# Attention chunks of a fused attention + two-MoE kernel: score products, y products and state products regrouped, and new durations for its list scheduler

## The chip, the cores and the metric

One core of one Trainium2 chip. The metric is the device time of one execution in microseconds (us), the median of several runs. Engines: PE (matrix multiply; "PEld" is its weight load, which overlaps the products), DVE (vector), ACT (scalar), POOL (general), SP (issues the DMAs).

## The reference

Three layers on 4 batches, 8 heads, 768 steps, 48 dimensions. The first is a linear recurrence with a complex decay:

```python
for t in range(S):
    new_re = ar * S_re - ai * S_im
    new_im = ar * S_im + ai * S_re
    S_re, S_im = (new_re + einsum('bhd,bhe->bhde', k[t], v[t]), new_im)
    y[t] = einsum('bhd,bhde->bhe', q[t], S_re)
```

Then a dense layer of width 2048 with a leaky rectifier, (3072 x 384) @ (384 x 2048) @ (2048 x 384), and then a layer with 8 experts of width 1024, of which each token uses one or none. All in float32.

## The kernel before

The recurrence is cut into 24 chunks, six of 128 steps for each of four batches; the number of a chunk is s = 4c + b. A chunk has two parts.

- `elementwise(s)` (E) loads a, q and k of the chunk into a tile X (two buffers), turns the decay into phases and magnitudes on ACT and DVE (two kinds of scan, line 416), and multiplies q and k by them. The results go through DRAM to be laid out anew: SP issues kd<-QP and qd<-X (write), then kh<-kd and qh<-qd (read back), and then the load of X for the chunk after next.
- `attention(s)` (P) forms, for two groups g of four heads, the 128 x 128 scores ("at", 4 products), masks them on DVE into A, transposes k ("at" again, 4 transposes) and copies it on ACT into kT, adds up y = v'A + St'q in the PSUM tile y, and forms the state products kT'v in the PSUM tile sps (one buffer, `s_ps`), which DVE adds to the state St and multiplies by the decay (su, then St). The last four chunks (c = 5) form no transposes and no state products, the first four (c = 0) have no St'q and no su.

A float32 product takes two passes on the tensor engine, so four products show as eight instructions. The y products go out by `columns`: each has 32 stationary columns, and four of them lie side by side in the array.

Each two chunks give 256 tokens to `moe_block(m)` (M, 12 of them): 8 pairs of F-blocks, each with 18 "h" products of 256 columns, ACT copies, DVE rectifies and splits (hs, gh, gl), and 12 "acc" products of 394 columns. The dense weights are decoded (d) in the first 120 us or so. After the last M comes the expert stage (loads r, items I), whose pools open when the attention pools and those of the dense layer close.

The order of all these instructions is written by a list scheduler, `Plan.emit`: it goes through a planned time, in which each recorded instruction has a duration (its `cost`), and at each step gives every engine the ready instruction with the lowest priority number. The result is a fixed order on every engine, and each engine then works through its order, waiting where an operand is late. The durations only set the order. Priorities come from `do_E`, `do_P`, `do_M`, `do_d` with lists of hand-set offsets; a chunk has four steps, `pri(0)` to `pri(3)`, and between two steps lies about one F-block pair of M. The planned end of a DMA is its bytes at a given rate plus 2 us (1.1 before it and 0.9 behind).

Of the kernel before, what the change touches and what calls it, by code (L numbers as in the profile page):

```python
# [57 lines left out]

# ---------------------------------------------------------------- list scheduler
class Buf:  # L60
    """A tile that is allocated when its first instruction is emitted."""

# [12 lines left out]
class View:  # L75
    """An access pattern on a Buf, resolved when its instruction is emitted."""

# [77 lines left out]
def real(x):  # L155
    return x.ap() if isinstance(x, View) else x
# [6 lines left out]
class Slots:  # L163
    """Buffers of one tag, taken in the order in which their first instructions are issued."""

# [20 lines left out]
class Plan:  # L186
    """Orders recorded instructions by priority as their operands become ready."""

    label = ''
    after = ()  # L190
# [17 lines left out]
    def gate(self, ops, fn):  # L208
        """Runs `fn` between `ops` and the instructions that name its result in `after`."""
        return self.add("NONE", 0.0, fn, after=ops)  # L210
# [152 lines left out]

# ---------------------------------------------------------------- kernel
def moe_kernel(tc, a, qk, v, w_in, w_out, alpha, w_gs, w1, w2, nat, nat_v, out):
# [7 lines left out]
    def cols(x):  # L373
        return x.cols if isinstance(x, View) else 0
# [40 lines left out]
    def scan(o, x, y, init, op1):  # L415
        dve(o, cols(o), lambda: nc.vector.tensor_tensor_scan(  # L416
            out=real(o), data0=real(x), data1=real(y), initial=real(init), op0=ALU.mult, op1=op1), [x, y, init])

    def mm(o, l, r, start, stop):
        n = cols(o)  # L420
        dt = l.dtype
        if dt == F32R:
            cost = max(n, 256) / 2.4 + 2.5
        elif dt == BF16:
            cost = 30
        else:
            cost = 2 * (max(n, 128) / 1.2 + (6 if n <= 128 else 0) if n > 64 else 213)
        pl.add("PE", cost / 1e3, lambda: nc.tensor.matmul(real(o), lhsT=real(l), rhs=real(r), start=start, stop=stop,  # L428
                                                          skip_group_check=True),
               [l, r] + ([] if start else [o]), [o])  # L430
# [27 lines left out]
    with ctx:  # L458
# [106 lines left out]
        def elementwise(s, pri):  # L565
# [44 lines left out]
            for x, name in ((1, "k"), (0, "q")):  # L610
                n = 129 if x else 128
                if x:
                    P = pl.buf(e1, [128, 6, 129], F32, "QP")
                    ts(P[:, :, 128].rearrange("p (c g) -> p c g", c=2), bc(GG[:, 127:384:128], 2), -0.5, ALU.mult)
                else:
                    P = X[:, 2:4, :].rearrange("p c (g t) -> p (c g) t", g=3)
                tt(P[:, :, 0:128].rearrange("p (c g) t -> p c g t", c=2),
                   X[:, 5 + x, :].rearrange("p (o g t) -> p o g t", o=1, g=3).to_broadcast([128, 2, 3, 128]), cs4, ALU.mult)
                d_ = pl.buf(drb, [6, 128, n], F32, name + "d", bufs=3)
                h_ = pl.buf(qp, [96, H, n], F32, name + "h", bufs=2) if x else qhs[s % 2][0:96, :, :]  # L620
                dma(d_.rearrange("x p t -> x p t"), P, 396e3)
                pl.ops[-1].fn = (lambda d=d_, P=P: nc.sync.dma_start(d.ap().rearrange("x p t -> p x t"), P.ap()))
                dma(h_, d_, 396e3)
                pl.ops[-1].fn = (lambda d=d_, h=h_: nc.sync.dma_start(
                    h.ap(), d.ap().rearrange("x (i h) t -> (x i) h t", h=H)))
                qk_of[s, x] = h_ if x else qhs[s % 2]

        def attention(s, pri):
# [10 lines left out]
            y = pbuf(y_ps, [128, 3, 128], "y")  # L639
            m4 = mask.rearrange("p (o f) -> p o f", o=1).to_broadcast([128, 4, 128])  # L640
            for g in range(2):
                pl.pri = pri(2 * g)
                at = pbuf(at_ps, [128, 512], "at", bufs=2)
                for x in range(4):
                    mm(at[:, x * 128:(x + 1) * 128], kh[:, 4 * g + x, 0:128], qh[0:96, 4 * g + x, :], True, True)
                A = pl.buf(pp, [128, 4, 128], F32, "A", bufs=2)
                tt(A, at.rearrange("p (x t) -> p x t", x=4), m4, ALU.mult)
                if not last:
                    at = pbuf(at_ps, [128, 512], "at", bufs=2)
                    for x in range(4):  # L650
                        transpose(at[:, x * 96:x * 96 + 96], kh[:, 4 * g + x, 0:128], ident[0:96, 0:96])
                    kT = pl.buf(pp, [128, 4, 96], F32, "kT", bufs=2)
                    copy(kT, at[:, 0:384].rearrange("p (x d) -> p x d", x=4))
                pl.pri = pri(2 * g + 1)
                ops = []
                for t, off in ((g, 32 * g), (2, 32 - 32 * g)):
                    for inter in range(c > 0, -1, -1):
                        for x in range(4):
                            h = 4 * g + x
                            cs = slice(h * 64 + off, h * 64 + off + 32)  # L660
                            ops.append((y[32 * x:32 * x + 32, t, :],) + (
                                (St[:, b, cs], qh[:, h, :]) if inter else (vt[:, cs], A[:, x, :])))
                columns(ops, g == 0)
                if last:
                    continue
                sps = pbuf(s_ps, [128, 512], "sps")[0:96, :]
                for x in range(4):
                    h = 4 * g + x
                    mm(sps[:, x * 128:x * 128 + 128], kT[:, x, :], vt[:, (h - g) * 64:(h - g) * 64 + 128],
                       True, True)  # L670
                new = sps.rearrange("p (h e) -> p h e", h=4)[:, :, 80 * g:80 * g + 48]
                sv = St[0:96, b, g * 256:g * 256 + 256].rearrange("p (h e) -> p h e", h=4)[:, :, 16 * g:16 * g + 48]
                gc = kh[:, 4 * g:4 * g + 4, 128:129].to_broadcast([96, 4, 48])
                if c:
                    su = pl.buf(pp, [96, 4, 48], F32, "su")
                    tt(su, new, sv, ALU.add)
                    tt(sv, su, gc, ALU.mult)
                else:
                    tt(sv, new, gc, ALU.mult)
# [3 lines left out]

        def columns(ops, fresh):
            """Products of 32 columns each, four of which the tensor engine carries side by side."""
            def go():
                for n, (o, l, r) in enumerate(ops):
                    ins = nc.tensor.matmul(real(o), lhsT=real(l), rhs=real(r), start=fresh and n < 4,
                                           stop=n >= len(ops) - 4, skip_group_check=True)
                return ins  # L690

            pl.add("PE", 0.0745 * len(ops), go, [x for op in ops for x in op[1:]], [op[0] for op in ops])

# [60 lines left out]
        def disjoint(group, ins, last):  # L754
            """The rows of one indirect write are not those of another: only the last one waits for them."""
            for other in group:
# [154 lines left out]
        def rank_experts(spare):  # L911
            """Order of the experts by their counts so far, and the slots each of them gets."""
            cnt = spare[0:1, 32:32 + E]
# [28 lines left out]
        def start_of(n):  # L942
            """Reads an item's expert and its first slot into registers."""
            r, _, col = ITEMS[n]
# [162 lines left out]
        def count_items(tp):  # L1107
            """Lists the (expert, first slot) of every 256 tokens beyond the first cap[e] of expert e."""
            cnt = scratch(tp)[:, 0:E]
# [29 lines left out]
        def check_inputs(tp):  # L1139
            """Sets the flag of the general path."""  # L1140
            good = tiny(tp, [128, NCHK + NF], "good")
# [12 lines left out]
        def finish():  # L1154
            """Tokens beyond the slots of their expert, after the general path if an input needs it."""
            pl.live = True
# [47 lines left out]
        def general():  # L1204
            """x1 and the routing without any assumption on the values: the recurrence step by step."""
            st = ExitStack()
# [148 lines left out]
        def filler():  # L1355
            """A product of constants that keeps the tensor engine's clock up while it waits for the first real ones."""
            if not idle:
# [134 lines left out]
```

## Time and profile before

| | |
|---|---|
| median of 3 runs | 811.39 us (808.46 to 816.9) |
| span of the profiled execution | 807.5 us |
| median of the runs less this span | 3.9 us |
| PE busy | 738.8 us, 91% of the span |
| DVE busy | 604.8 us, 75% |
| ACT busy | 498.4 us, 62% |
| last y products issued | 632.7 us |
| PE clock granted, mean | 0.981 |

The profile has the span, from the first to the last instruction; the run's own time is not given beside it, so the sum is made against the span, and 3.9 us are added to come to the median. Matmuls overlap, so that the step from one start to the next, and not the duration of one, is what a product costs the engine.

### The profile page before, as it was taken

How to read it: one execution, taken by the hardware profiler on the slowest of the kernel's cores; microseconds unless marked ns; L12 is line 12 of the kernel's file. 1: busy time of each engine (PE TensorE's matmuls, PEld its weight loads, DVE VectorE, ACT ScalarE, POOL GpSimd, SP SyncE). 2: the span in 40 equal slices, each digit the busy share in tenths (PEclk: the TensorE clock that was granted, in tenths of full speed). 3: DMA queues.
4: the chain of work that ended last, by engine and by line, in shares of the span. 5: the costliest groups of instructions: out<-in, count | busy, mean ns of one | idle time of the engine just before them, and what ended most of it. 6: DMA issues, size and time to landing. Idle time of an engine off the chain costs nothing.

```text
span 807.5 us, 16491 instructions
## 1 busy us (share of the span) xinstructions
PE 738.8 (91%) x6322; PEld 698.8 (87%) x6322; DVE 604.8 (75%) x1460; ACT 498.4 (62%) x839; POOL 70.5 (9%) x118
## 2 busy tenths in 40 slices
PE   1689899989999998999999999989999999999993
PEld 0578789979889998999998998889999999899993
DVE  5979989978879897887867788677873473676741
ACT  7769759666847785577777567586652362555530
POOL 4000000100000010010100101001000203710110
PEclk9989999999999999999999999999999999999997
DMA  6585665767484776525334542535340432599400
GB/s 232 164 261 170 216 209 175 216 193 236 109 275 122 212 213 203 145 70 166 112 114 131 158 129 76 142 101 135 116 132 2 165 126 84 187 395 390 155 11 18
DMA packets 86983, 130.53 MB, mean 162 GB/s; under 512 B 8822, under 2 KB 60096, under 8 KB 86896
## 3 DMA queue, kind: packets, MB, share of 16 engines
q1 hardware_dynamic: 84336, 125.35, 50.9%
q0 software_dynamic: 2560, 4.05, 1.6%
q8 instruction: 52, 0.85, 0.5%
q14 instruction: 35, 0.29, 0.2%
HBM read 99.46 MB, written 31.29 MB: 162 GB/s over the span
## 4 chain that ended last, share of the span: by engine, by line
DVE 28%; PE 28%; DMA 25%; ACT 12%; issue 4%; SPq 1%; POOL 0%; POOLq 0%; ACTq 0%; DVEq 0%
PE h L428 13%; PE acc L428 12%; DMA X<-in_a 9%; DMA qd<-X 7%; DVE X L397 6%; DVE hs L405 3%; ACT X L385 3%; DVE X L416 3%; DVE X L405 3%; ACT L357 3%; DMA qh<-qd 2%; DVE gl L397 2%; ACT Rr L385 2%; DVE QP L397 1%; DVE chk L412 1%
## 5 line engine op out<-in xcount | busy, mean ns | idle before, releaser
L428 PE MATMUL h<-xhi,wih 128*128 128x256 f32 x576 | 168.3, 293 | 1.1 <-ACT wih L390 0.7
L428 PE MATMUL h<-xlo,wih 128*128 128x256 f32 x576 | 164.3, 285 | 0.3 <-DVE xlo L397 0.2
L428 PE MATMUL h<-xhi,wil 128*128 128x256 f32 x576 | 163.4, 284 | 0.0
L385 ACT ACTIVATE X<-X 128x384 f32<-128x384 f32 (+1 forms) x216 | 117.8, 558 | 66.7 <-DMA X<-in_a 44.3
L428 PE MATMUL acc<-woh,gh 128*128 128x394 f32 x384 | 135.4, 353 | 8.4 <-ACT gh L390 8.2
L428 PE MATMUL acc<-wol,gh 128*128 128x394 f32 x384 | 132.7, 346 | 0.0
L428 PE MATMUL acc<-woh,gl 128*128 128x394 f32 x384 | 130.8, 353 | 1.5 <-DVE gl L397 1.1
L428 PEld LDWEIGHTS h<-xhi,wih 128*128 128x128 f32 x576 | 110.0, 191 | 3.0 <-issue 1.0
L428 PEld LDWEIGHTS h<-xlo,wih 128*128 128x128 f32 x576 | 110.2, 191 | 0.8 <-DVE xlo L397 0.7
L428 PEld LDWEIGHTS h<-xhi,wil 128*128 128x128 f32 x576 | 110.2, 191 | 0.1
L405 DVE SCALAR_TENSOR_TENSOR hs<-hs,alp 128x256 f32<-128x256 f32 x192 | 86.6, 479 | 31.0 <-ACT hs L390 30.6
L390 ACT CAST gh<-hs 128x512 fp32r<-128x512 f32 x96 | 59.0, 615 | 68.2 <-DVE hs L405 61.0
L357 ACT ACT_TABLE_LOAD x77 | 98.8, 1283 | 1.2
L428 PEld LDWEIGHTS acc<-woh,gh 128*128 128x128 f32 x384 | 73.1, 191 | 12.7 <-ACT gh L390 11.2
L390 ACT COPY hs<-h 128x512 f32<-128x512 f32 x96 | 55.5, 578 | 45.0 <-PE h L428 41.8
L397 DVE TENSOR_TENSOR gl<-hs,gh 128x512 fp32r<-128x512 f32 x96 | 65.8, 686 | 18.5 <-ACT gh L390 18.2
L856 POOL DMA_INDIRECT lst<-tok,ix x24 | 26.5, 1106 | 605.4 <-DVE ix L401 601.8
L428 PEld LDWEIGHTS acc<-woh,gl 128*128 128x128 f32 x384 | 71.5, 191 | 6.0 <-DVE gl L397 5.0
L397 DVE TENSOR_TENSOR X<-X 128x768 f32<-128x768 f32 (+1 forms) x96 | 72.0, 751 | 5.9 <-ACT X L385 5.7
L428 PEld LDWEIGHTS acc<-wol,gh 128*128 128x128 f32 x384 | 73.5, 191 | 0.1
L428 PE MATMUL at<-qh,kh 96*128 96x128 f32 x384 | 54.4, 281 | 15.7 <-DMA qh<-qd 15.7
L428 PEld LDWEIGHTS at<-qh,kh 96*128 96x128 f32 x384 | 50.4, 195 | 17.6 <-issue 16.3
(186 smaller groups left out, 1406.0 us busy)
## 6 DMA issues: line engine op xcount, KB each, us to landing
r<-in_w SPq DMA_DIRECT2D x24, 512.0 KB, 6.3
r<-in_w SPq DMA_DIRECT2D x32, 384.0 KB, 9.6
kd<-QP SPq DMA_DIRECT2D x24, 387.0 KB, 4.6
kh<-kd SPq DMA_DIRECT2D x24, 387.0 KB, 3.7
X<-in_a SPq DMA_DIRECT2D x24, 384.0 KB, 5.6
X<-in_qk SPq DMA_DIRECT2D x24, 384.0 KB, 6.1
qd<-X SPq DMA_DIRECT2D x24, 384.0 KB, 4.1
qh<-qd SPq DMA_DIRECT2D x24, 384.0 KB, 5.0
```

The costliest lines, as they stand in the source:

```text
L357: nc.scalar.preload_act_table_set(o)
L385: lambda: nc.scalar.activation(real(o), real(i), f, **{k: real(x) for k, x in kw.items()}),
L390: lambda: nc.scalar.copy(real(o), real(i)), [i], [o])
L397: dve(o, cols(o), lambda: nc.vector.tensor_tensor(out=real(o), in0=real(x), in1=real(y), op=op), [x, y], late=late)
L405: dve(o, cols(o), lambda: nc.vector.scalar_tensor_tensor(out=real(o), in0=real(x), scalar=real(s), in1=real(y), op0=op0, op1=op1), [x, y, s])
L412: dve(o, cols(i), lambda: nc.vector.tensor_reduce(out=real(o), in_=real(i), axis=AX.X, op=op, apply_absolute_value=absolute), [i])
L416: dve(o, cols(o), lambda: nc.vector.tensor_tensor_scan(out=real(o), data0=real(x), data1=real(y), initial=real(init), op0=ALU.mult, op1=op ...
L428: pl.add("PE", cost / 1e3, lambda: nc.tensor.matmul(real(o), lhsT=real(l), rhs=real(r), start=start, stop=stop, skip_group_check=True), [l ...
L856: r = nc.gpsimd.indirect_dma_start(out=lst, out_offset=bass.IndirectOffsetOnAxis(ap=real(ix[:, t:t + 1].bitcast(U32)), axis=0), in_=toks[t ...
```

## The change

In `attention`, the loop over the two head groups is cut in three: first scores, mask and transposes of both groups (steps 0 and 1), then one call of `columns` with the y products of both groups (step 2, all St'q first and then all v'A), and then the state products of both groups (step 3). A state product moves 96 columns of v and not 128, and `new` is cut out of the narrower result. The number of tensor instructions stays the same.

The scheduler gets other durations: scans 2n-16 columns and not n, float32r products 13.5 ns and not 2.5 ns beside their columns, float32 products by the larger of moving and stationary columns, the four transfers through DRAM 650 KB and 520 KB worth of time and not 396 KB, and a stretch of n y products 0.3 + 0.0575 n us and not 0.0745 n. The lists of priority offsets stay as they were. Comments are taken out elsewhere.

```diff
     def scan(o, x, y, init, op1):
-        dve(o, cols(o), lambda: nc.vector.tensor_tensor_scan(
+        dve(o, 2 * cols(o) - 16, lambda: nc.vector.tensor_tensor_scan(
...
         if dt == F32R:
-            cost = max(n, 256) / 2.4 + 2.5
+            cost = max(n, 256) / 2.4 + 13.5
         elif dt == BF16:
             cost = 30
         else:
-            cost = 2 * (max(n, 128) / 1.2 + (6 if n <= 128 else 0) if n > 64 else 213)
+            cost = 2 * (max(n, math.prod(l.shape[1:])) / 1.2 + (6 if n <= 128 else 0))
...
-                dma(d_.rearrange("x p t -> x p t"), P, 396e3)
+                dma(d_.rearrange("x p t -> x p t"), P, 650e3)
...
-                dma(h_, d_, 396e3)
+                dma(h_, d_, 520e3)
...
+            As, kTs = [], []
             for g in range(2):
-                pl.pri = pri(2 * g)
+                pl.pri = pri(g)
                 at = pbuf(at_ps, [128, 512], "at", bufs=2)
...
-                pl.pri = pri(2 * g + 1)
-                ops = []
-                for t, off in ((g, 32 * g), (2, 32 - 32 * g)):
-                    for inter in range(c > 0, -1, -1):
+            pl.pri = pri(2)
+            ops = []
+            for inter in range(c > 0, -1, -1):
+                for g in range(2):
+                    for t, off in ((g, 32 * g), (2, 32 - 32 * g)):
                         for x in range(4):
                             h = 4 * g + x
                             cs = slice(h * 64 + off, h * 64 + off + 32)
                             ops.append((y[32 * x:32 * x + 32, t, :],) + (
-                                (St[:, b, cs], qh[:, h, :]) if inter else (vt[:, cs], A[:, x, :])))
-                columns(ops, g == 0)
-                if last:
-                    continue
+                                (St[:, b, cs], qh[:, h, :]) if inter else (vt[:, cs], As[g][:, x, :])))
+            columns(ops)
+            pl.pri = pri(3)
+            for g in range(0 if last else 2):
                 sps = pbuf(s_ps, [128, 512], "sps")[0:96, :]
                 for x in range(4):
                     h = 4 * g + x
-                    mm(sps[:, x * 128:x * 128 + 128], kT[:, x, :], vt[:, (h - g) * 64:(h - g) * 64 + 128],
+                    mm(sps[:, x * 128:x * 128 + 96], kTs[g][:, x, :], vt[:, h * 64 - 32 * g:h * 64 - 32 * g + 96],
                        True, True)
-                new = sps.rearrange("p (h e) -> p h e", h=4)[:, :, 80 * g:80 * g + 48]
+                new = sps.rearrange("p (h e) -> p h e", h=4)[:, :, 48 * g:48 * g + 48]
...
-            pl.add("PE", 0.0745 * len(ops), go, [x for op in ops for x in op[1:]], [op[0] for op in ops])
+            pl.add("PE", 0.3 + 0.0575 * len(ops), go, [x for op in ops for x in op[1:]], [op[0] for op in ops])
```

## Rows read from the trace of the kernel before

**Rows 1.** The page: busy time of each engine, and granted clock by slice.

```profile
PE 738.8 (91%) x6322; PEld 698.8 (87%) x6322; DVE 604.8 (75%) x1460; ACT 498.4 (62%) x839; POOL 70.5 (9%) x118
...
PEclk9989999999999999999999999999999999999997
```

**Rows 2.** Busy time by stage: time, then PE, PEld, DVE, ACT, POOL, clock, DMA.

```profile
50.00:634.00 584.00, 557.02 (x5029) 521.73 (x5028) 470.37 (x1152) 390.34 (x664) 22.89 (x21) 0.99 0.52 153
...
100.00:150.00 50.00, 48.31 (x402) 45.22 (x403) 46.90 (x120) 37.08 (x69) 2.28 (x2) 1.00 0.62 182
...
550.00:600.00 50.00, 49.59 (x480) 46.70 (x479) 37.90 (x95) 30.87 (x50) 2.08 (x2) 1.00 0.48 132
```

**Rows 3.** PE's waits from 50 to 634 us: total, times, longest.

```profile
PE at L428 <- DMA qh<-qd: 12.7, 8, 2.8
PE acc L428 <- ACT gh L390: 8.2, 9, 1.9
```

**Rows 4.** Chain that ended last, shares by line, of 50:590 and of 590:634.

```profile
by line: DMA X<-in_a 12.3%; DMA qd<-X 8.3%; DVE X L397 7.7%; DVE hs L405 5.0%; ACT X L385 4.9%; issue 4.6%; DVE X L416 4.2%; ACT L357 4.0%; DVE X L405 3.7%; DMA qh<-qd 3.6%; PE acc L428 3.6%; PE h L428 3.2%; DVE gl L397 3.1%; ACT Rr L385 2.
...
by line: PE h L428 41.1%; PE acc L428 40.3%; PE y L688 9.3%; DMA ids<-lst 7.2%; PE at L428 6.1%; ACT gh L390 1.2%; issue 0.3%; SPq L991 0.1%
```

**Rows 5.** PE in order of time, one group of a chunk: start, duration.

```profile
500.89 0.34 PE L428 MATMUL acc<-wol,gh 128*128 128x394 f32 x1
501.06 0.34 PE L428 MATMUL acc<-woh,gl 128*128 128x394 f32 x1
501.33 0.42 PE L688 MATMUL y<-qh,St 128*32 128x128 f32 x8
501.57 0.40 PE L688 MATMUL y<-A,vt 128*32 128x128 f32 x8
501.79 0.40 PE L688 MATMUL y<-qh,St 128*32 128x128 f32 x8
502.01 0.40 PE L688 MATMUL y<-A,vt 128*32 128x128 f32 x8
502.34 1.11 PE L428 MATMUL sps<-vt,kT 128*96 128x128 f32 x8
503.21 0.36 PE L428 MATMUL h<-xhi,wih 128*128 128x256 f32 x1
...
507.63 1.05 PE L428 MATMUL at<-qh,kh 96*128 96x128 f32 x8
508.52 0.49 PE L433 MATMUL at<-ident,kh 96*128 96x96 f32 x4
508.80 0.36 PE L428 MATMUL h<-xhi,wih 128*128 128x256 f32 x1
```

**Rows 6.** PE in the decode stage, products of 10 moving columns, and what follows.

```profile
94.69 0.73 PE L428 MATMUL at<-wgs,wt 128*128 128x10 f32 x6
95.28 0.89 PE L428 MATMUL at<-Ao,ident 128*128 128x384 f32 x2
```

**Rows 7.** Weight loads by shape: busy, mean ns of one, idle before.

```profile
L428 PEld LDWEIGHTS at<-qh,kh 96*128 96x128 f32 x384 | 50.4, 195 | 17.6 <-issue 16.3 <-DMA qh<-qd 1.3
L428 PEld LDWEIGHTS sps<-vt,kT 128*96 128x96 f32 x320 | 37.2, 163 | 5.9 <-issue 4.2 <-ACT Rr L385 0.6 <-ACT wih L390 0.4
L688 PEld LDWEIGHTS y<-A,vt 128*32 128x32 f32 x768 | 22.9, 113 | 2.1 <-DVE A L397 0.7 <-issue 0.5 <-DVE wol L397 0.3
```

**Rows 8.** DVE's read of the state products, and another set of them on PE.

```profile
503.49 0.35 DVE L397 TENSOR_TENSOR su<-sps,St 96x192 f32<-96x192 f32 x1
...
281.45 0.34 DVE L397 TENSOR_TENSOR su<-sps,St 96x192 f32<-96x192 f32 x1
...
277.92 1.11 PE L428 MATMUL sps<-vt,kT 128*96 128x128 f32 x8
```

**Rows 9.** DMA issues: KB each, median us to landing.

```profile
qd<-X SPq DMA_DIRECT2D x24, 384.0 KB, 4.1
qh<-qd SPq DMA_DIRECT2D x24, 384.0 KB, 5.0
```

**Rows 10.** DVE's scans by shape: busy, mean ns of one, idle before.

```profile
L416 DVE TENSOR_TENSOR_SCAN X<-X,Rr 128x128 f32<-128x128 f32 x72 | 26.7, 408 | 0.4
L416 DVE TENSOR_TENSOR_SCAN X<-hole,X 128x384 f32<-128x384 bf16 x24 | 22.8, 949 | 0.2
```

**Rows 11.** The expert weights' loads (durations ns, first and last start), and POOL's wait.

```profile
L959 SPq DMA_DIRECT2D r<-in_w x56: 332/373/1307, 637.3 to 755.0; - x56
...
POOL xg L998 <- PE y L688: 30.1, 1, 30.1
```

More of the change, by code (lines that the diff above doesn't have):

```diff
@@ L647, in attention @@
                 tt(A, at.rearrange("p (x t) -> p x t", x=4), m4, ALU.mult)
+                As.append(A)
                 if not last:
@@ L653, in attention @@
                     copy(kT, at[:, 0:384].rearrange("p (x d) -> p x d", x=4))
-                pl.pri = pri(2 * g + 1)
-                ops = []
-                for t, off in ((g, 32 * g), (2, 32 - 32 * g)):
-                    for inter in range(c > 0, -1, -1):
+                    kTs.append(kT)
+            pl.pri = pri(2)
[3 more added lines that the diff above has]
+                    for t, off in ((g, 32 * g), (2, 32 - 32 * g)):
                         for x in range(4):
@@ L682, in attention, with columns @@
             tt(xlo[:, :, cs], y, xhi[:, :, cs], ALU.subtract)
-        def columns(ops, fresh):
+        def columns(ops):
             def go():
                 for n, (o, l, r) in enumerate(ops):
-                    ins = nc.tensor.matmul(real(o), lhsT=real(l), rhs=real(r), start=fresh and n < 4,
+                    ins = nc.tensor.matmul(real(o), lhsT=real(l), rhs=real(r), start=n < 4,
                                            stop=n >= len(ops) - 4, skip_group_check=True)
                 return ins
-            pl.add("PE", 0.0745 * len(ops), go, [x for op in ops for x in op[1:]], [op[0] for op in ops])
+            pl.add("PE", 0.3 + 0.0575 * len(ops), go, [x for op in ops for x in op[1:]], [op[0] for op in ops])
         def decode64(src, n, name):
```

## The prediction

> **What bounds the kernel now.** I read the page's busy times first: PE 91% of the span, DVE 75%, ACT 62% [rows 1]. An average over stages says little, so next came the busy times by stage, for the stage that holds all that the change touches, from 50 us (first chunks) to 634 us (last y products). There PE is busy for 557.0 of 584 us, 95%, and no other engine comes near it over the stage; only at 100 to 150 us is DVE as full (46.9 of 50 us, PE 48.3), and at the end of the stage PE is alone (49.6 of 50, DVE 37.9) [rows 2]. The granted clock is 1.00 or close to it in these stretches, the upper of its two levels, so no part of the time is a slow clock. PE's waits in the stage are few: 12.7 us for the read-back of q (8 times) and 8.2 us for gh from ACT (9 times) make up nearly all of its idle time [rows 3].
>
> The chain of waits speaks a second language. Before 590 us it runs mostly through the E part (loads of X, the transfers through DRAM, DVE and ACT on X), and h and acc together hold under 7% of it; from 590 to 634 us PE's h and acc hold 81% [rows 4]. So up to 590 us two paths are nearly tied: PE's full queue, and the elementwise pipeline that feeds it and meets it at the wait for q. I take PE as the bound, since it has only 27 us idle in 584, but count part of each PE saving as lost.
>
> **State products: 96 moving columns for 128.** Twenty chunks (the last four have none) x 2 groups x 4 heads x 2 passes are 320 instructions. Eight of them take 503.21 - 502.34 = 0.87 us of PE's time, 109 ns each [rows 5]. What sets 109 ns? The score products, with the same 128 moving columns but 128 stationary ones, take (508.52 - 507.63)/8 = 111 ns [rows 5], although their weight load is longer, 195 ns against 163 [rows 7]. So in the state products the moving columns decide, and a cut of a quarter shortens the pass to 82 ns if it is in proportion. The weight load then comes close: it grows by 163 - 113 = 50 ns from 32 to 96 stationary columns [rows 7], 0.78 ns a column, which for 96 is 75 ns, just below. I take 83 ns: 320 x 26 ns = 8.3 us of PE time saved. The bounds: ten moving columns still take (95.28 - 94.69)/6 = 98 ns with 128 stationary ones [rows 6]; if that were a floor for float32 passes of any width, the saving is 320 x 11 ns = 3.5 us. Transposes with 96 moving columns take (508.80 - 508.52)/4 = 70 ns [rows 5]; at that, 12.5 us. My value is nearest to the width that was itself traced, scaled.
>
> The Trainium skill ("TensorE: Matmul & The Clock Gate", section "LDWEIGHTS (loading the stationary operand)") has the load cost the number of stationary columns divided by 1.2, in ns, whatever their depth. That would be 80 ns for the 96 columns here, before and after the change, and a floor for the new pass; by it the saving would be at most 320 x 29 ns = 9.3 us as an estimate, against the 12.5 us that the transposes allow. The trace neither confirms nor denies the figure for float32, since no pass with 96 stationary and fewer moving columns ran.
>
> **y products in one stretch.** The work is the same 64 instructions for a chunk (32 in the first four), in one block and not two. What is saved is a change of shape. The first y group starts 0.27 us after the last acc product where acc products are 0.17 to 0.18 apart: 0.09 too late. The y groups of eight are then 0.24, 0.22 and 0.22 apart, and the state products follow the last by 0.33: 0.02 and 0.11 more [rows 5]. Together 0.22 us for each entry and exit, once less in each of 24 chunks: 5.3 us. Bounds: nothing, if such a change costs only where PE has a full queue and the planner splits something else in its stead, and 24 x 0.33 = 7.9 us, if the whole last step is the drain. The row shows one undisturbed block, so I take 5.3.
>
> **How much of that arrives.** 8.3 + 5.3 = 13.6 us of PE time. Three of the 20 chunks with state products lie before 125 us, where DVE is as full as PE, and after that PE must still meet the elementwise path. I count 85%, 11.6 us; the bounds are nothing and the whole. After 634 us the expert stage starts when the attention and dense pools close: the first expert load goes out at 637.3 us, and POOL waits 30.1 us for the last y product [rows 11]. So what is saved ahead of it moves that stage forward as a whole; no operation of it is changed.
>
> **The new wait.** Both groups of state products are now at one step, and there is one PSUM buffer for them. The second group's products cannot start before DVE's su has read the first. Before, about two steps with some 8 us of F-block products lay between. Now the planner sees PE free while it waits for su, and puts in h or acc products for the time that it thinks su takes; if DVE is later than planned, PE stands at the second group with the rest of its queue behind it: h, acc, and by them hs on ACT. In the trace su ends 503.84 - 503.21 = 0.63 us after PE leaves the state products in one chunk [rows 5, 8], and 281.79 - 278.8 = 3.0 us in another (state products from 277.92, 0.87 us of PE's time; DVE is full there) [rows 8]. With perfect filling the wait costs nothing; with none, some 1.4 us (between these two, nearer to the short one) x 20 = 28 us. I expect the filling to be off by 0.2 us a chunk: 4 us, because all durations of DVE that matter in it, the scans, are now planned as they run.
>
> **The other moves.** y of group 0 goes one step later and y of group 1 one step earlier. xhi and xlo, which M needs, come after group 1, so they come a step earlier, and qh of the chunk is free a step earlier; both cost nothing. Both A buffers and both kT buffers are now held until steps 2 and 3; the next chunk wants them at its own step 0, a step of about 4.3 us after step 3, so ACT's copy of the next kT can stand behind the second state products, with hs and gh queued behind it. That is nothing as long as PE is not more than a step late. No DMA is moved in the code itself; SP's order can change only through the plan.
>
> **The durations.** They move nothing by themselves, but the order comes from them. The plan ran one F-block pair at 18 x 109 + 12 x 167 = 3.97 us and now runs it at 4.30; a group of y and state products was planned at more than its 2 us. It landed each transfer of q after 1.1 + 1.1 + 0.9 = 3.1 us, where the trace has 4.1 and 5.0 [rows 9]; now 3.8 and 3.4, which makes up 1.0 of the 2.9 us that the two were short. The short scans were planned at 202 ns and the long one at 469, which run 408 and 949 as busy time [rows 10]; now 319 and 852. So q's read-back should be asked for a little earlier, relative to PE, than now. Of the 12.7 us [rows 3] a quarter, 3 us, might go. The bounds are wide: at best the waits for q and gh of rows 3 all go, 20.9 us; at worst, since the hand-set priority offsets stay as they were while the times under them change, the same waits double, 20.9 us lost.
>
> **The sum.** 807.5 - 11.6 + 4 - 3 = 796.9 us of span. The median of the runs lies 3.9 us above the profiled span, which gives 801 us, 10 less than before (1.3%).
>
> **The rivals.**
> 1. The elementwise path holds the stage. For it: the chain before 590 us [rows 4]. Against it: PE's idle time is just 5% there [rows 2], and ACT and DVE have idle time to catch up. PE's savings then turn into longer waits for q, only the stretch from 590 us on gains (four chunks at 0.22 us), and with 4 us for the new wait hidden too the time is 807 to 814 us, say 810.
> 2. The new wait decides, and the kernel is slower. The place is the second group of state products, in 20 chunks. Its price is the wait less what the planner fills; it decides from 14.6 / 20 = 0.73 us of unfilled wait a chunk (11.6 and 3 us are what it has to eat up). At 1.4 us unfilled it is 28 us, 811.4 - 14.6 + 28 = 825 us. For it: su was 3 us late in a full stretch [rows 8], and DVE stays above 90% there. Against it: the same order puts PE work there, and only DVE's lateness against the plan counts.
> 3. The planned times now fit so much better that PE's stalls shrink by half (10 us of the 20.9) and the new wait is filled wholly: 811.4 - 13.6 - 10 = 788 us.
> 4. The narrower pass is no shorter than the floor of rows 6 allows: 3.5 for 8.3 us saved, the sum then is 805 us. It is part of the spread about the forecast.
>
> **How the numbers follow.** Chances: my sum, with its spread of 794 to 806 us, 0.42; rival 3 (below 794) 0.15; rival 1 (806 to 815) 0.25; rival 2 (above 815) 0.18. About 1% (8.1 us) is what a measurement of this kernel tells from no change, the three runs before being 8.4 us apart. Faster by that means below 803.3 us: all of rival 3 and nearly nine tenths of the forecast's spread, 0.52. Slower means above 819.5: most of rival 2, 0.15. Between them 0.33. For 8 in 10, the range leaves out 1 in 20 below and 3 in 20 above: 785 to 820 us.
>
> **What would show it.** State products eight to about 0.67 us in PE's order of time (0.78 or more: rows 6 were the floor). One y block of 64 instructions, about 1.9 us long, in each chunk of c > 0. Waits of PE's state products for DVE's su, 4 us in all in the table of waits; over 15 us is rival 2. Waits of the scores for q below 12.7 us; if they grow to 20 while PE's busy time falls by 13, it is rival 1. The last y product at about 622 us in place of 632.7, and the expert stage as long as before. The prediction is wrong above all if the new order changes the elementwise part's place against M, for which the trace of before has no row.

## The result, and the profile after

The changed kernel takes 801.37 us (median of 20 runs, 795.08 to 811.15), the kernel before 812.06 us beside it (20 runs, 807.41 to 820.12). The ratio is 0.9865, 95% interval 0.9839 to 0.9892: 1.35% faster, 11 us. The forecast was 801 us. The runs below show that this number came out of several wrong terms whose errors cancel. A profile shows one execution, and executions of one kernel differ by more than 1%, so times are compared by medians; the profile of the kernel before is of an execution quicker than its median, and that of `narrow`, shown below, of one slower than its median.

The span of the profiled execution is 800.3 us, 7.2 us less than before. Its page, to be read beside [rows 1]:

```profile
PE 729.4 (91%) x6368; PEld 702.9 (88%) x6368; DVE 610.2 (76%) x1460; ACT 508.7 (64%) x847; POOL 69.7 (9%) x118
...
PEclk9999999999989999999999999999999999999997
```

PE is busy 9.4 us less, DVE 5.4 us and ACT 10.3 us more. PE's 46 more instructions are not attention: the plan puts filler products of constants on PE where it sees it idle between 27 and 55 us of its planned time, and there are 106 of them now and 60 before. ACT's eight more are loads of its function tables (85 for 77 at line 357, 1.28 us each), which follow from the order too. So the durations set a little more than the order. The waits of PE from 50 to 634 us, against [rows 3]:

```profile
PE at L428 <- DMA qh<-qd: 13.3, 8, 3.9
PE acc L428 <- ACT gh L390: 5.0, 5, 1.4
PE acc L428 <- DVE gl L397: 3.5, 4, 1.4
PE sps L428 <- DVE su L397: 2.3, 2, 1.3
```

The wait for q is not shorter (12.7 us before). The new wait is there, in two of 20 chunks. In PE's order of time, one chunk of the changed kernel, against [rows 5]:

```profile
455.33 1.08 PE L692 MATMUL y<-qh,St 128*32 128x128 f32 x32
456.23 1.06 PE L692 MATMUL y<-A,vt 128*32 128x128 f32 x32
457.21 0.39 PE L428 MATMUL h<-xhi,wih 128*128 128x256 f32 x1
...
461.63 0.84 PE L428 MATMUL sps<-vt,kT 128*96 128x96 f32 x8
462.25 0.36 PE L428 MATMUL h<-xhi,wih 128*128 128x256 f32 x1
```

The y stretch takes 457.21 - 455.33 = 1.88 us in one piece, where the two pieces took 1.01 us each; a state pass takes (462.25 - 461.63)/8 = 78 ns, where it took 109. Both are what was forecast or a little better (the 109 is looked at again below). The chain before 590 us keeps its kind, transfers and elementwise work with h and acc under 9% [rows 4]:

```profile
by line: DMA X<-in_a 11.1%; ACT X L385 8.3%; DVE X L397 7.5%; DMA qd<-X 6.1%; DMA qh<-qd 5.7%; ACT L357 5.4%; issue 4.5%; PE acc L428 4.5%; PE h L428 4.2%; DVE X L405 3.3%; DVE hs L405 3.1%; PE at L428 2.9%; DVE gl L397 2.6%; DMA kd<-QP 2.6
```

The expert stage starts earlier, and the first expert load with it (637.3 us before [rows 11]):

```profile
L963 SPq DMA_DIRECT2D r<-in_w x56: 332/373/1415, 629.9 to 748.4; - x56
```

The last y product starts at 620.3 us, where 622 was forecast and 632.7 measured before, but it is no fair mark, since group 1's y products went one step forward in the order. A better one is the last "acc" product of the dense layer, 672.5 us before and 663.7 after: 8.8 us won up to there; behind it 135 and 137 us remain.

### The profile page after: what moved, and what is told of

It reads as the page before. It is cut to its first block, busy times and chain, and to the rows that moved or that the text cites. A ratio compares the mean times of both kernels' runs of the same rounds, so it can differ in the third digit from the quotient of the medians.

```text
span 800.3 us, 16598 instructions
## 1 busy us (share of the span) xinstructions
PE 729.4 (91%) x6368; PEld 702.9 (88%) x6368; DVE 610.2 (76%) x1460; ACT 508.7 (64%) x847; POOL 69.7 (9%) x118
## 4 chain that ended last, share of the span: by engine, by line
PE 27%; DMA 25%; DVE 21%; ACT 16%; issue 8%; SPq 2%; POOL 1%; POOLq 0%; ACTq 0%; DVEq 0%
PE h L428 10%; PE acc L428 10%; DMA X<-in_a 7%; ACT X L385 6%; DVE X L397 5%; DMA qh<-qd 5%; DMA qd<-X 4%; ACT L357 4%; PE at L428 3%; DVE X L405 2%; DVE hs L405 2%; DVE gl L397 2%; DMA kd<-QP 2%; DMA rawc<-in_w_out 2%; PE y L692 2%
## 5 line engine op out<-in xcount | busy, mean ns | idle before, releaser
L397 DVE TENSOR_TENSOR X<-X 128x384 f32<-128x384 f32 (+1 forms) x96 | 72.1, 751 | 11.2 <-ACT X L385 10.6
L428 PE MATMUL at<-qh,kh 96*128 96x128 f32 x384 | 57.1, 293 | 17.0 <-DMA qh<-qd 16.6
L428 PEld LDWEIGHTS at<-qh,kh 96*128 96x128 f32 x384 | 53.2, 206 | 19.1 <-issue 10.9
```

Source lines behind the costliest of these rows:

```text
L397: dve(o, cols(o), lambda: nc.vector.tensor_tensor(out=real(o), in0=real(x), in1=real(y), op=op), [x, y], late=late)
```

## The experiments

Three groups of four kernels ran, each group on one chip beside the kernel before, which took 814.4, 815.1 and 806.2 us there (medians). So times are compared as ratios to the kernel before of the same group; 0.001 is 0.8 us.

**The change taken apart.** The first group undid or did one part alone.

`narrow` puts only the narrower state products into the kernel before. The planned cost is the same there for 96 and 128 columns, so the order of the instructions on every engine stays that of before.

```diff
-                    mm(sps[:, x * 128:x * 128 + 128], kT[:, x, :], vt[:, (h - g) * 64:(h - g) * 64 + 128],
+                    mm(sps[:, x * 128:x * 128 + 96], kT[:, x, :], vt[:, h * 64 - 32 * g:h * 64 - 32 * g + 96],
...
-                new = sps.rearrange("p (h e) -> p h e", h=4)[:, :, 80 * g:80 * g + 48]
+                new = sps.rearrange("p (h e) -> p h e", h=4)[:, :, 48 * g:48 * g + 48]
```

> The kernel before with 96 moving columns in the state products and nothing else; the order of the instructions on every engine stays that of before. Theory (PE's work is what counts, and nearly all of it arrives): eight passes take 0.62 us and not 0.87, 320 x 31 ns = 10 us of PE time, of which 85% arrive: 8 us faster, some 803 us where before is 812. Rival 1 (the elementwise path holds the stage up to 590 us): at most 2 us faster. Rival 2 (the gain of the change comes from the new durations and the order they make): at most 3 us faster.

Measured: ratio 1.0023 (0.9993 to 1.0053). No gain at all, although the passes are as narrow as in the changed kernel. My theory, that 85% of PE's saving arrives, fell here.

`group` is the changed kernel with 128 columns and all old durations; `group_narrow` the same with 96 columns; `durations` is the kernel before with all new durations and nothing else:

```diff
-        dve(o, cols(o), lambda: nc.vector.tensor_tensor_scan(
+        dve(o, 2 * cols(o) - 16, lambda: nc.vector.tensor_tensor_scan(
...
-            cost = max(n, 256) / 2.4 + 2.5
+            cost = max(n, 256) / 2.4 + 13.5
...
-            cost = 2 * (max(n, 128) / 1.2 + (6 if n <= 128 else 0) if n > 64 else 213)
+            cost = 2 * (max(n, math.prod(l.shape[1:])) / 1.2 + (6 if n <= 128 else 0))
...
-                dma(d_.rearrange("x p t -> x p t"), P, 396e3)
+                dma(d_.rearrange("x p t -> x p t"), P, 650e3)
...
-                dma(h_, d_, 396e3)
+                dma(h_, d_, 520e3)
...
-            pl.add("PE", 0.0745 * len(ops), go, [x for op in ops for x in op[1:]], [op[0] for op in ops])
+            pl.add("PE", 0.3 + 0.0575 * len(ops), go, [x for op in ops for x in op[1:]], [op[0] for op in ops])
```

> The kernel before with the new grouping alone (both groups' scores, then one y stretch, then both groups' state products), 128 moving columns and the old durations. Theory: 24 x 0.22 = 5 us of PE time saved in the y stretches, 85% of it arrives, and the wait of the second state products for su takes back 2 to 5 us: between no change and 3 us faster. Rival 2: no change, or slower since the durations do not fit the new order. Rival 3 (the order that the scheduler happens to write is worth several us either way, so the parts do not add up): anything from 10 us faster to 10 us slower.

> The changed kernel with the old durations: the new grouping and 96 moving columns. Theory: 8 to 11 us faster than before, near the whole change. Rival 1 and rival 2: 0 to 3 us faster. Rival 3: does not equal the sum of the two parts by themselves by several us.

> The kernel before with the new durations of the scheduler alone; every instruction is the same, only the order changes. Theory: 0 to 4 us faster, the waits of the scores for q not clearly shorter (they were 12.7 us before and 13.3 after). Rival 2: 8 us faster or more. Rival 3: anything from 10 us faster to 10 us slower.

Measured: `group` 1.0179 (1.0154 to 1.0204), `group_narrow` 1.0186 (1.0146 to 1.0227), `durations` 0.9887 (0.9857 to 0.9917). So the new grouping under the old durations is 15 us slower, narrower passes do not help it, and the durations alone, which change no instruction of the layers (38 fillers and 8 table loads come with their order), bring 9 of the 11 us. The waits of PE in `group`, 50 to 634 us:

```profile
PE at L428 <- DMA qh<-qd: 21.3, 11, 3.1
...
PE sps L428 <- DVE su L397: 3.8, 4, 1.8
PE sps L428 <- DVE St L397: 2.6, 1, 2.6
```

The wait for q grew by 8.6 us and the second state products wait 6.4 us: the new wait, and a later q. The clock has a share as well: the mean granted clock of the six executions of `group` is 0.964, that of the kernel before beside it 0.978, and 0.014 x 829 us is up to 12 us of full clock lost (an estimate). How the 15 us divide between these waits, the clock and the mere order was not tested.

**The pass width in a better order, and which duration.** My second theory was that PE's savings are lost in the order of before, where the elementwise part sets the pace, and count in the order that the new durations write. `dur_narrow` is `durations` with 96 columns in the order of `durations`; `after_wide` is the changed kernel with 128 columns in the order of the changed kernel (the planned cost is kept at the old value in the one, at that of 96 columns in the other). The edits are those of `narrow`, the second backwards.

> The kernel before with the new durations and 96 moving columns, old grouping; the order on every engine is that of the run with the durations alone. New theory (in the order of before the elementwise path sets the pace, so PE's savings vanish; the new durations make the chunks' spacing even and leave PE as the bound from about 325 us on): now the narrower passes count in the stage after 325 us, about 12 of 20 chunks x 0.5 us = 6 us, so 5 to 7 us below the durations alone, 796 to 800 us against 812 to 814. Rival (PE's savings vanish in this order too): the same as the durations alone within 2 us, and the rest of the whole change's gain comes from the grouping.

> The changed kernel with 128 moving columns in the state products and the same planned order as the changed kernel. New theory: 5 to 8 us slower than the changed kernel, ratio to before 0.993 to 0.997; it is then no better than the durations alone, so the grouping gives nothing. Rival: within 2 us of the changed kernel, ratio 0.985 to 0.989.

Measured: `dur_narrow` 0.9895 (0.9855 to 0.9935), against 0.9887 without; `after_wide` 0.9854 (0.9814 to 0.9894), against 0.9865 with 96 columns. Twice no gain from the narrower pass; each of these comparisons goes across chips and can hide some 4 us. The second theory fell too, at least in the size that it gave. And `after_wide` against `durations` is all that the grouping can have brought under the new durations: 0.9854 against 0.9887, 3 us with an uncertainty of some 4 us.

`dur_f32r` takes over the 13.5 ns of the float32r products alone, `dur_rest` all new durations but that one.

> The kernel before with one new duration, that of the float32r products (13.5 ns beside the columns in place of 2.5). New theory (the plan ran PE some 8% too fast in the dense layer, so it gave the elementwise steps too late a place beside it; this one number mends that): 6 to 10 us faster than before. Rival (the scans and the transfers through DRAM are what was planned wrong on the path that sets the pace): no change, within 3 us.

> The kernel before with all new durations except that of the float32r products. New theory: no change within 3 us, or slower. Rival: 6 to 10 us faster than before.

Measured: `dur_f32r` 1.0120 (1.0077 to 1.0162), `dur_rest` 0.9929 (0.9893 to 0.9965). The number that I held for the cause makes the kernel slower by itself; scans, transfers through DRAM, float32 products and y stretches bring 6 us without it, and both together 9. In `dur_f32r` PE waits elsewhere (50 to 634 us):

```profile
PE acc L428 <- DVE gl L397: 9.4, 8, 3.4
PE acc L428 <- ACT gh L390: 6.7, 8, 2.9
PE at L428 <- DMA qh<-qd: 4.7, 3, 2.6
```

The q wait is the smallest of all runs here but the waits for gh and gl, which stood at 8.2 and 1.1 us in the kernel before, are 16.1 us together. My reading, which no run tests, is that the elementwise work came so early in the order of DVE and ACT that the dense layer's own splits came late.

**How much is the order itself worth?** Two kernels move one planned duration by 1 ns and nothing else: `after_f12` has 12.5 for 13.5 in the changed kernel, `before_f3` 3.5 for 2.5 in the kernel before.

```diff
-            cost = max(n, 256) / 2.4 + 13.5
+            cost = max(n, 256) / 2.4 + 12.5
```

> The changed kernel with 12.5 ns in place of 13.5 beside the columns of a float32r product in the plan; every instruction is the same, only the order changes. Theory (the gain is one of durations near the trace, so a neighbour of them is about as good): ratio to before 0.982 to 0.993. Rival (each small step of a duration writes another order, good or bad by luck): off by more than 6 us from the changed kernel, below 0.979 or above 0.994.

> The kernel before with 3.5 ns in place of 2.5 beside the columns of a float32r product in the plan. Theory: ratio to before 0.993 to 1.007. Rival (luck of the order): off by more than 6 us either way.

Measured: `after_f12` 0.9944 (0.9907 to 0.9981), `before_f3` 1.0156 (1.0106 to 1.0205). The one is 6 us off the changed kernel, the other 13 us off the kernel before. The rival is right in the second case; in the first the ratio is outside what the theory gave and just inside what the rival gave. A step of 1 ns in a plan can move this kernel by as much as the whole change did.

**The new wait, and the pass's floor.** `apart` puts the first group's state products a step earlier than the second's. `one_bank` forms 64 columns for each head, all eight heads in the one PSUM bank, and DVE adds and multiplies 512 columns at once:

```diff
             for g in range(0 if last else 2):
+                pl.pri = pri(2 + g)
                 sps = pbuf(s_ps, [128, 512], "sps")[0:96, :]
```

```diff
+            if not last:
+                sps = pbuf(s_ps, [128, 512], "sps")[0:96, :]
+                states([(sps[:, h * 64:h * 64 + 64], kTs[h // 4][:, h % 4, :], vt[:, h * 64:h * 64 + 64]) for h in range(H)])
+                new = sps.rearrange("p (h e) -> p h e", h=H)
+                sv = St[0:96, b, :].rearrange("p (h e) -> p h e", h=H)
+                gc = kh[:, :, 128:129].to_broadcast([96, H, 64])
+                if c:
+                    tt(sv, new, sv, ALU.add)
+                    tt(sv, sv, gc, ALU.mult)
+                else:
+                    tt(sv, new, gc, ALU.mult)
```

> The changed kernel with the first group's state products one step earlier (with the y stretch) and the second group's where they are, so that some 4 us of dense products lie between them and the wait for su goes. Theory: the wait of 2.3 us in the table of waits goes to nothing, and the time stays within 4 us of the changed kernel, since the gap is mostly filled. Rival (the wait costs more than the table shows, by what queues behind it): 5 us or more faster than the changed kernel, ratio below 0.980. Luck of the order could also show as anything above 0.993.

> The changed kernel with 64 moving columns in each state product, all eight heads side by side in the one PSUM bank, and one DVE addition and one multiplication over 512 columns in place of two of 192 each: no wait between the two groups. If the load of 96 stationary columns bounds the pass, eight passes stay at 0.62 us; if the moving columns do, they take 0.45 us and PE saves 20 x 2 x 0.17 = 7 us more. Theory: PE savings come back as waiting for the most part, so within 5 us of the changed kernel either way. Rival (the wait and PE's work count in full): 5 to 9 us faster than the changed kernel, ratio 0.975 to 0.980.

Measured: `apart` 0.9898 (0.9860 to 0.9936), `one_bank` 0.9842 (0.9772 to 0.9912). In `apart` the wait is all but gone, and the time is that of the changed kernel or a little above:

```profile
PE sps L428 <- DVE su L397: 0.3, 1, 0.3
```

So taking away 2.3 us of wait in the table brought nothing that can be measured, and the rival's 5 us lie outside this interval. But `apart` also writes another order, and an order alone was worth up to 13 us above, so a gain that a worse order hides is not excluded. `one_bank` has the lowest ratio of all, but its interval holds that of the changed kernel; it beats the kernel before, and whether it beats the changed one stays open. Its passes:

```profile
454.26 1.49 PE L687 MATMUL sps<-vt,kT 128*96 128x64 f32 x16
455.57 0.36 PE L428 MATMUL h<-xhi,wih 128*128 128x256 f32 x1
```

Sixteen passes take 455.57 - 454.26 = 1.31 us, 82 ns each with 64 moving columns, and 78 ns with 96. With 96 stationary columns, fewer than 96 moving ones no longer shorten the pass.

## Why the number was right and the reasons were not

**Where PE's saving went.** The busy time by stage, from 50 us to the end of the dense layer, for the pairs that differ in the pass width alone and have one order (columns as in [rows 2]). Of the kernel before:

```profile
50.00:672.90 622.90, 595.02 (x5295) 559.16 (x5294) 493.49 (x1207) 409.60 (x696) 27.45 (x25) 0.99 0.52 153
```

`narrow`:

```profile
50.00:683.30 633.30, 597.49 (x5300) 560.24 (x5298) 493.93 (x1208) 410.53 (x695) 27.44 (x25) 0.98 0.51 150
```

`after_wide`:

```profile
50.00:668.10 618.10, 592.82 (x5336) 569.79 (x5328) 496.33 (x1205) 419.73 (x702) 27.40 (x25) 0.98 0.53 154
```

The changed kernel:

```profile
50.00:664.10 614.10, 584.95 (x5332) 561.65 (x5321) 495.73 (x1205) 418.76 (x703) 28.07 (x25) 0.99 0.53 155
```

In the changed kernel PE is busy 7.9 us less than with wide passes, but idle 614.1 - 585.0 = 29.1 us against 25.3: half of the saving comes back as waiting in these two executions, and the medians show none of the rest. In `narrow` it is worse: PE idles 35.8 us against 27.9, and its busy time is not even lower, at a granted clock of 0.98 against 0.99. (The 10 us between these two stages are more than the medians show; that no gain is left is what both say.) This fits rival 1 of the prediction, that the elementwise path takes up what PE saves; which instructions take it up was not followed.

In `narrow` the clock takes a share too. Over all executions the mean granted clock is 0.973 there and 0.978 in the kernel before beside it, and 0.005 x 817 us is up to 4 us of full clock lost (an estimate). But the loss does not need the clock: `durations` and `dur_narrow` both have a mean of 0.982, and the narrower pass gains nothing there either.

**What the durations mend.** The instructions on X (on ACT and DVE) that stand idle for the load of X show it. Idle time before them, total and times, in the view of that tile; the kernel before:

```profile
  DMA X<-in_a: 75.3, 33
```

`group`:

```profile
  DMA X<-in_a: 66.0, 25
```

`dur_f32r`:

```profile
  DMA X<-in_a: 61.2, 26
```

`dur_rest`:

```profile
  DMA X<-in_a: 16.7, 13
```

`durations`:

```profile
  DMA X<-in_a: 42.5, 23
```

The changed kernel:

```profile
  DMA X<-in_a: 39.0, 27
```

X's buffer comes free when qd<-X has landed, and on SP the next load of X stands behind kh and qh, which wait for kd and qd. As long as the plan lands those too early, it puts the first instruction of the next chunk at a place in ACT's and DVE's order where X has not come, and the engine stands there with hs, gh and gl queued behind it. All 14 kernels with a profile fall into two sets: with the old durations of transfers and scans (and of y stretches and float32 products, which went with them) these waits are 52.6 to 80.3 us (before, `narrow`, `group`, `group_narrow`, `dur_f32r`, `before_f3`), and every ratio is 1.000 or above; with the new ones 16.7 to 42.5 us (the other eight), and every ratio is 0.9944 or below. That this wait is the cause is argued from the two sets; transfers and scans were not tried apart, nor was this wait taken out by itself. Within a set it does not order the kernels: `dur_rest` has the least and is not the quickest.

The fillers divide the 14 kernels into the same two sets: 60 of them with the old durations, 98 or 106 with the new ones. Their line among the groups of instructions, in the kernel before and in the changed one:

```profile
L1359 PE MATMUL acc<-ident 128*128 128x128 f32 x60 | 9.8, 319 | 0.0
```

```profile
L1363 PE MATMUL acc<-ident 128*128 128x128 f32 x106 | 15.6, 309 | 0.0
```

No run tries them by themselves, but the traces show that the time is won later. All fillers start before 63 us. The acc products of woh with gh are 384 in each kernel. The 192nd starts at 389.9 us in the kernel before, and later than that in `durations` (396.8) and in the changed kernel (392.9); the 288th starts at 547.7, 543.6 and 537.9 us. Between these two marks the waits of X's instructions for its load shrink, and with them PE's for gh. The kernel before, 390 to 548 us (a line of the view of X, then one of PE's waits):

```profile
  DMA X<-in_a: 28.6, 11
PE acc L428 <- ACT gh L390: 5.9, 6, 1.9
```

The changed kernel, 393 to 538 us:

```profile
  DMA X<-in_a: 7.5, 8
PE acc L428 <- ACT gh L390: 0.3, 1, 0.3
```

So in these executions the stretch in which the time is won is the one in which X's load is waited for less, which supports the reading and does not prove it.

**Point by point.**

- State products, pass width: mis-sized, by its starting point. The pass is 78 ns where 83 was taken, but the 109 ns of [rows 5] were of a block right behind y products. Behind acc products eight passes with 128 columns take 0.79 us, 99 ns each, in the kernel before (from 338.29 to 339.08 us) and in `after_wide`:

```profile
465.09 1.03 PE L428 MATMUL sps<-vt,kT 128*96 128x128 f32 x8
465.88 0.37 PE L428 MATMUL h<-xhi,wih 128*128 128x256 f32 x1
```

  Like with like the narrower pass saves 21 ns, and 320 x 21 ns = 6.7 us, not 8.3. There is a floor, which 64 moving columns do not pass. The Trainium skill ("TensorE: Matmul & The Clock Gate", "LDWEIGHTS (loading the stationary operand)") has the load at 96 columns / 1.2 = 80 ns, and the blocks shown above take 78 to 82 for 96 and for 64 moving columns. That the load is the floor is not shown: 128 stationary columns would be 107 ns by the same rule (an estimate), and [rows 5] and [rows 6] have 70 ns for transposes and 98 ns for products of 10 moving columns.
- One y stretch: 2 x 1.01 + 0.09 less 1.88 is 0.23 us for a chunk, as worked out (0.22).
- "How much of that arrives", 85%: the step that failed, above all. In the order of before nothing arrives (ratio 1.0023 where 0.991 was expected), in the two later orders nothing that can be measured. I had seen that the chain before 590 us runs through the elementwise part and let the 95% of PE overrule it.
- The new wait, 4 us: 2.3 us in the table; `apart`, which takes it away, is no quicker. In the old durations' order it is 6.4 us, beside a later q and a lower clock in a 15 us loss. The rival that has it decide is not right for the changed kernel; for `group` it stays open.
- The durations, 3 us by an earlier q: mis-sized threefold. They bring 9.2 us alone (0.0113 x 814.4). In `durations` PE's wait for q is 9.2 us, 3.5 us shorter than before and so of the size forecast, but that leaves most of the gain; in the changed kernel it is no shorter (13.3 us). Rival 3, which had the waits of [rows 3] halve, is nearest for the durations, but in the changed kernel these fall only from 20.9 to 18.3 us. The prediction said that their effect had no row in the trace of before; the waits of X's instructions for its load had one, and I did not read it.
- The sum: 11.6 us of PE time did not arrive, and in their place stand 4 us of wait for which no cost was seen and 6 us more from the durations. The errors cancel to within 2 us: the number was right by luck.

What stays open: which of transfers, scans and fillers does it, whether the grouping gains anything under the new durations (3 us, not told from none), and how much of any of these ratios is the fit of the plan and how much the one order that it happens to write, given what 1 ns does in `before_f3`.

## What to carry to other kernels

Where a planner writes the order of several in-order engines, the busiest engine is not the bound just because it is 95% busy: take one part out in the same order and see whether its saving arrives. When planned durations change, look for the instruction that stands idle at the head of its queue for a transfer, on whichever engine, since everything behind it waits too. And try a neighbouring plan before one part of a gain is put down to anything: here 1 ns in one duration was worth up to 13 us.

## What the hardware showed that I had not expected

A single wait can be paid twice. In the changed kernel PE waits 3.86 us for q at 153 us, and the eight score passes behind it take 159.15 - 157.28 = 1.87 us where others take 0.9 (PE in order of time):

```profile
157.28 2.08 PE L428 MATMUL at<-qh,kh 96*128 96x128 f32 x8 [3.86 <-DMA qh<-qd]
159.15 0.85 PE L433 MATMUL at<-ident,kh 96*128 96x96 f32 x4
...
201.50 1.05 PE L428 MATMUL at<-qh,kh 96*128 96x128 f32 x8
202.40 0.49 PE L433 MATMUL at<-ident,kh 96*128 96x96 f32 x4
```

The granted clock shows why (last but two columns in the busy times by stage):

```profile
153.50:157.20 3.70, 0.00 (x0) 0.00 (x0) 2.73 (x6) 2.66 (x4) 0.00 (x0) 0.99 1.03 316
157.20:163.90 6.70, 6.62 (x33) 6.62 (x33) 4.99 (x11) 3.35 (x6) 0.00 (x0) 0.50 0.30 98
163.90:170.00 6.10, 6.10 (x53) 6.07 (x51) 3.86 (x9) 3.30 (x5) 0.00 (x0) 1.00 0.30 86
```

PE did nothing from 153.4 to 157.2 us; then it was busy, but until 163.9 us at 0.50 of full clock, the lower of the two levels (1.2 GHz for 2.4), and after that at 1.00. 6.7 us at half speed do the work of 3.35 us, so the wait of 3.86 us cost about 3.3 us more behind it (an estimate).
